# Attention with a relative bias and a squared-ReLU network on one core: v as fp32 by another queue, and one more batch turned by DMA

## The chip, the core and the metric

The kernel runs on one core of a Trainium2 chip. The metric is the device time of one execution, in microseconds (us); the time before is 378.62 us, the median of three runs (378.29 to 379.13). The profile is that of one execution, whose instructions span 376.3 us. The core's engines have these names in it: PE is TensorE (matrix multiplies; PEld is its loading of weights), ACT is ScalarE, DVE is VectorE, POOL is GpSimd and SP is SyncE, which here does nothing but issue transfers.

## The reference

Eight batches, eight heads, 576 positions, heads of 64. Attention with a bias that depends on the distance of two positions alone, then a layer 512 to 2048, a ReLU, a square, and a layer 2048 to 512, for all 4608 tokens:

```python
def _attn_ref(q, k, v, bias_table):          # (8, 8, 576, 64); table (32, 8); all fp32
    scores = scale * np.matmul(q, k.transpose(0, 1, 3, 2))
    bucket = ...                             # of |i - j|; one bucket from distance 128 on
    bias = bias_table[bucket]
    scores = scores + bias.transpose(2, 0, 1)[None, :, :, :]
    attn = np.exp(scores - max); attn = attn / (sum + 1e-09)      # cut: over the last axis
    return np.matmul(attn, v)

def _moe_ref(x, w_in, w_out):                # x (4608, 512), w_in (512, 2048), w_out (2048, 512)
    h = np.maximum(x @ w_in, 0.0)
    return h * h @ w_out
```

## The kernel before

The kernel works in fp16 with fp32 sums. Two heads make a *pair*: four pairs a batch, 32 in all. For each pair, q and k are laid with the head dimension on the partitions (they are *turned*), TensorE makes the scores (tile `st`), ScalarE takes exp (into `pt`, and `pm` for the last 64 keys), VectorE multiplies by the table of exp(bias) where it differs from a constant, TensorE multiplies by v (tile `pv`), and VectorE divides by the sums (tile `x`). x is turned again (into `xt`) for the network, which runs in nine *layers* of 512 tokens: f1 (L1044) with w_in, a ReLU into `rt`, a square into `g`, and f2 (L962) with w_out in seven products instead of eight, for which VectorE makes sums of quarters of the weights and of the activations.

All work is first entered in a plan, with estimated durations; a list scheduler puts it in order, and each engine's instructions are emitted in that order. So the order on every engine is fixed in the program, and constants that steer the plan (when a pair or a layer is due) change the order everywhere.

```python
DT_QK = 3                                    # q, k are turned by DMA from this batch on
PERIOD, LEAD, FAST, FASTN = 9600.0, 1600.0, 3000, 7      # when pair p is due, in planned ns
AHEAD, G0, GP = 20600.0, 54700.0, 35900.0    # layer g is due at G0 + GP * g
DT_X = 3                                     # x is turned by DMA from this batch on
RELU_DVE = 2                                 # in layers below this, VectorE may take a ReLU
SIX = 3                                      # batches below this: q, k loaded six rows to a partition
ORDER = "k0 i0 q0 q1 v i1 i2 o0 k1 o1 i3 o2 o3"   # q, k, v of batch 1 and the weights (i: w_in, o: w_out)
...
def nominal(p):
    return LEAD + FAST * min(p, FASTN) + PERIOD * max(p - FASTN, 0)
```

The loads are issued by GpSimd's queue, which casts fp32 to fp16 on the way. A pair of a batch below SIX is one transfer for q and one for k, with long rows; from SIX on it is three each, row by row, in the form that a DMA transpose takes. A batch of v is four transfers into `va` and two into `vm` (last 64 keys):

```python
def load_six(p, w):
    ... src.rearrange("h (p j) d -> p h (j d)", j=6) ...

def load_rows(p, w):
    ... [src[e, 0:512, :].rearrange("(t p) d -> p t d", p=128) for e in range(2)] ...
    ... [src[:, 512:S, :].rearrange("e p d -> p e d")] ...

def load_v(b):
    for tt in range(4):
        l = load("POOL", nc.gpsimd, lambda tt=tt: vas[b_v[b].slot][:, tt, :, 0:64],
                 const(v[b, :, ts(tt, 128), :].transpose([1, 0, 2])), ...)
    load_v_tail(b)                           # two transfers into vm
```

Turning q and k, and x:

```python
def pair(p):
    for w, dst in ((0, qts), (1, kts)):
        if b >= DT_QK:
            nc.sync.dma_start_transpose(out=dst[...], in_=stg[b_stg[p].slot][w][:, 0:640])   # by SyncE
            continue
        # else TensorE (L608), 12 transposes if b < SIX, into PSUM tile f
        nc.tensor.transpose(ps[ds(64 * e, 64), ts(j, 96)], six(t)[:, e, ts(j, D)], id_sb[0:96, 0:96])
        # and ScalarE or VectorE copies PSUM to qt / kt (L570, L572)
    # copies of the last 64 queries and keys into qz (L635): GpSimd, or for b < DT_QK VectorE or GpSimd
    ...
    if b >= DT_X:
        nc.sync.dma_start_transpose(out=xt_sb[...], in_=xs[...])        # 2 a pair, by SyncE

def x_turn(b, norms):                        # for b < DT_X, by TensorE (L848)
    for qt in range(5):
        for kk in range(4):
            nc.tensor.transpose(ps[:, ts(kk, 128)], xs[xb[kk].slot][:, qt, :], id_sb)
        # then a copy to xt by ScalarE or VectorE
```

Of the kernel before, what the change touches and what calls it, by code (L numbers as in the profile page):

```python
# [10 lines left out]
FP32 = mybir.dt.float32  # L11
# [6 lines left out]
B, H, S, D = 8, 8, 576, 64  # L18
# [8 lines left out]
NG = B * S // GT  # L27
XB = 3
XR = XB * S
DT_QK = 3  # L30
PERIOD, LEAD, FAST, FASTN = 9600.0, 1600.0, 3000, 7
AHEAD, G0, GP = 20600.0, 54700.0, 35900.0
DT_X = 3
RELU_DVE = 2
NSTG, NQK, NPT, NV, NX, NGB, NRT, NY = 5, 4, 3, 3, 6, 2, 4, 4
QUIET, LATER = 5200.0, 8500.0
TAB, EV = 6400.0, 1
P_ORDER = "1 6 2 5 7 3 4"
P_LAST = "1 6 2 5 7 3 4"
SIX = 3  # L40
ORDER = "k0 i0 q0 q1 v i1 i2 o0 k1 o1 i3 o2 o3"
HALF = GT // 2


# [133 lines left out]
def mm(n):  # L178
    return n / 2.4 + 2.5


def act(n):
    return 174.0 + n / 1.2


def dve(n, rate=1.0, fix=160.0):
    return fix + n / (0.96 * rate)
# [3 lines left out]
def kernel(  # L191
# [10 lines left out]
    nc = tc.nc  # L202
    assert (_bucket(np.arange(128, S)) == NBK - 1).all()

    def io(ins):
        tc.keep_in_program_order(ins)
        return ins
# [11 lines left out]
    def sb(name, shape, dtype=FP16):  # L219
        return single.tile(shape, dtype, name=name)  # L220
# [4 lines left out]
    w_out_sb = sb("w_out_sb", [128, 16, 512])  # L225
# [1 line left out]
    tm_sb = sb("tm_sb", [128, 4, 192])  # L227
    bt_sb = sb("bt_sb", [128, 8], FP32)
    far_sb = sb("far_sb", [1, 8], FP32)
    one_sb = sb("one_sb", [1, 128], FP32)  # L230
    ex_sb = sb("ex_sb", [128, 8])
    eb_sb = sb("eb_sb", [128, 4, 8])
    oh_sb = sb("oh_sb", [128, 512])
    stg = [[sb(f"{n}s{i}", [128, 12 * D]) for n in "qk"] for i in range(NSTG)]
    qts = [sb(f"qt{i}", [128, 640]) for i in range(NQK)]
    kts = [sb(f"kt{i}", [128, 640]) for i in range(NQK)]
# [6 lines left out]
    vas, v4s = ([t[:, i] for i in range(NV)] for t in (va_sb, vm_sb))  # L243
# [2 lines left out]
    wt_sb = sb("wt", [128, 3, 8, 256])  # L246
    ss = {i: sb(f"s{i}", [128, 8, 2, 128]) for i in (1, 2, 4)}
    gs = [sb(f"g{i}", [128, 16, GT]) for i in range(NGB)]
    rts = [sb(f"rt{i}", [128, GT]) for i in range(NRT)]
    ys = [sb(f"y{i}", [128, 512], FP32) for i in range(NY)]  # L250
    rs = [sb(f"r{i}", [128, 3, 2, 1], FP32) for i in range(2)]
# [5 lines left out]
    P = Plan()  # L257
# [5 lines left out]

    def loader(eng_name, eng, out_, in_, packets, deps=(), bufs=(), due=0.0):

        lane = [Buf(r_lane)] if eng_name == "POOL" else []
        issue = P.add(
            {eng_name: 720.0 if eng_name == "POOL" else 600.0},  # L270
            lambda: io(eng.dma_start(out=out_(), in_=in_())),  # L271
            deps,
            list(bufs) + lane,
            due,
        )
        return P.add({"DMA": packets / 16}, None, [issue], list(bufs) + lane, due if lane else -1e9), issue

    def one_of(engs, fn, deps, bufs, due):
        op = P.add(engs, None, deps, bufs, due)
# [3 lines left out]
    def const(f):  # L283
        return lambda: f

    def load(eng_name, eng, out_, in_, packets, deps=(), bufs=(), due=0.0):
        return loader(eng_name, eng, out_, in_, packets, deps, bufs, due)[0]


    first_f = gs[NGB - 1].bitcast(FP32).rearrange("p t c -> p (t c)")  # L290
# [6 lines left out]
        for w, (n, e, t) in enumerate((("SP", nc.sync, q), ("ACT", nc.scalar, k)))  # L297
# [22 lines left out]
        due=5,  # L320
# [20 lines left out]
                out=eb_sb, in0=sel_sb, in1=ex_sb.rearrange("p (a h) -> p a h", a=1).to_broadcast([128, 4, 8]), op=MULT  # L341
# [5 lines left out]
    for c in range(6):  # L347
# [11 lines left out]
        o = P.add({"PE": 16 * 55.0}, t_mm, [o_eb, l_oh], [t_b], LEAD + TAB, 0.0, "f")  # L359

        def t_ev(o, c=c, t_b=t_b):
# [4 lines left out]
            else:  # L366
# [8 lines left out]
                    out=tm_sb[ds(64 * e, 64), :, :], in_=tb_sb[ds(64 * e, 64), e::2, 64 * e : 64 * e + 192]  # L375
# [11 lines left out]
    def fill(ap, value, ns, due, after, deps=()):  # L387
        return P.add({"DVE": ns}, lambda: io(nc.vector.memset(ap, value)), deps, (), due, after)
# [7 lines left out]
    v_fix = [  # L396
        [
            o,
            fill(va_sb[:, a, :, :, 64:66], VSC, 150.0, 30, at),
            *(fill(vm_sb[ds(64 * e, 64), a, :, e, 64:66], VSC, 90.0, 30, at, [o]) for e in range(2)),  # L400
        ]
        for a, ns, at in ((slice(0, 1), 250.0, QUIET), (slice(1, NV), 500.0, LATER))
        for o in [fill(vm_sb[:, a].bitcast(FP32), 0.0, ns, 30, at)]
    ]
# [5 lines left out]

    b_v = [Buf(r_v) for _ in range(B)]
    l_qk = {}
    l_v = {}
    pool_due = [0.0]

    def pdue():
        pool_due[0] += 1.0
        return pool_due[0]  # L420
# [62 lines left out]
    def load_v_tail(b):  # L483
        for e in range(2):
            l = load(
                "POOL", nc.gpsimd,
                lambda e=e: v4s[b_v[b].slot][ds(64 * e, 64), :, e, 0:64],
                const(v[b, e::2, 512:576, :].transpose([1, 0, 2])),
                256 * 34.5, v_fix[min(b, 1)], [b_v[b]], pdue(),
            )  # L490
            for hp in range(4):
                l_v.setdefault((b, hp), []).append(l)

    def load_v(b):
        for tt in range(4):
            l = load(
                "POOL", nc.gpsimd,
                lambda tt=tt: vas[b_v[b].slot][:, tt, :, 0:64],
                const(v[b, :, ts(tt, 128), :].transpose([1, 0, 2])),
                1024 * 34.5, v_fix[min(b, 1)], [b_v[b]], pdue(),  # L500
            )
            for hp in range(4):
                l_v.setdefault((b, hp), []).append(l)
        load_v_tail(b)

    l_win, l_wout = [], []

    def load_w_in(u):
        l_win.append(
# [6 lines left out]
        )  # L516

    def load_w_out(u):
        l_wout.append(
            load(  # L520
                "POOL", nc.gpsimd,
                const(w_out_sb[:, 4 * u : 4 * u + 4, :]),
                const(moe_w_out[ds(512 * u, 512), :].rearrange("(a p) c -> p a c", p=128)),
                512 * 102, (), (), pdue(),
            )
        )

    for hp in range(4):
        for w in range(2):
# [9 lines left out]
    for h in range(6, 8):  # L539
        load_v_head(0, h)  # L540
    for step in ORDER.split():
        if step[0] == "i":
# [8 lines left out]
    for b in range(2, B):  # L551
        for p in range(4 * b, 4 * b + 4):
            for w in range(2):
                (load_six if b < SIX else load_rows)(p, w)
        load_v(b)

    def nominal(p):
        return LEAD + FAST * min(p, FASTN) + PERIOD * max(p - FASTN, 0)  # L560

    xt_ready, x_last = {}, {}
    x_bufs = {}
# [16 lines left out]
    def pair(p):  # L580
# [5 lines left out]
        for w, dst in ((0, qts), (1, kts)):  # L586
            if b >= DT_QK:
                o = P.add(
# [12 lines left out]
            def tr(w=w, bank=bank):  # L601
                ps = g_ps[bank.slot].bitcast(FP16)
                t = stg[b_stg[p].slot][w]
                if b < SIX:
                    for j in range(6):
# [10 lines left out]

            o = P.add({"PE": 12 * 36.0 if b < SIX else 5 * mm(128)}, tr, l_qk[p, w] + [l_id], [bank, b_stg[p]], T - 3000, after, "c" if b < SIX else "f")

            def turned(bank=bank):
                ps = g_ps[bank.slot].bitcast(FP16)[:, 0:S]  # L620
                return ps.rearrange("p (j t) -> p t j", j=6) if b < SIX else ps

            def straight(dst=dst):
                d = dst[qb.slot][:, 0:S]
                return d.rearrange("p (t j) -> p t j", j=6) if b < SIX else d

            evac.append(copy_to(S, straight, turned, [o], [bank, qb], T - 3000, b >= SIX, 0 < p < EV))
        spread = []
        for w, src, dst in ((0, qts, qzs), (1, kts, kzs)):
            for e in range(2):  # L630
# [5 lines left out]

                spread.append(one_of({"DVE": 200.0, "POOL": 320.0} if b < DT_QK else {"POOL": 320.0}, sp, [evac[w]] + z_fix[min(p, 1)], [qb], T - 1000))
        pb = Buf(r_pt)
# [132 lines left out]
        for part, qt0, nq in ((0, 0, 3), (1, 3, 2)):  # L771
# [48 lines left out]
            norms.append(o)  # L820
            if b >= DT_X:
                c = (b % XB) * S + 128 * qt0
# [61 lines left out]
    def sums_of_weights():  # L884

        done = []
        for c0 in (0, 4):
            cs = ds(c0, 4)
            l = [l_wout[c0 // 2], l_wout[c0 // 2 + 1]]
            t2, t3, t4 = (wt_sb[:, i, cs] for i in range(3))  # L890
            w11, w12, w21, w22 = (w4[:, cs, o, h] for o in range(2) for h in range(2))
            o = None
            for out_, a, b_, op in (
                (t3, w22, w12, mybir.AluOpType.add),
                (w12, w12, w11, mybir.AluOpType.subtract),
                (t2, w22, w12, mybir.AluOpType.add),
                (t4, w21, t2, mybir.AluOpType.subtract),
            ):
                o = P.add(
                    {"DVE": dve(1024, 2.0)},  # L900
                    lambda out_=out_, a=a, b_=b_, op=op: io(nc.vector.tensor_tensor(out=out_, in0=a, in1=b_, op=op)),
                    l + [o], (), 1e5,
                )
            done.append(o)
        return done
# [23 lines left out]
    def second(g):  # L929
# [22 lines left out]
        atoms = []  # L952
        for i in (int(x) for x in (P_LAST if g == NG - 1 else P_ORDER).split()):
            bk, left, right, ns = prod[i]
# [71 lines left out]
    def layers(g):  # L1026
# [27 lines left out]
        for i in range(16):  # L1054
            if i < len(atoms1):
# [12 lines left out]

                engs = {"ACT": act(512), "DVE": dve(512)} if g < RELU_DVE else {"ACT": act(512)}
                r = one_of(engs, relu, [o], [bank, rb], 0.0)  # L1070
# [26 lines left out]
    for b in range(B):  # L1097
        norms = [pair(4 * b + hp) for hp in range(4)]
        if b < DT_X:
            x_turn(b, norms)  # L1100
# [38 lines left out]
```

The softmax here doesn't subtract the row's maximum and nothing guards it: scores larger than these inputs give would overflow.

## Time and profile before

| what | value |
|---|---|
| time, median of 3 runs | 378.62 us |
| span of the profiled execution | 376.3 us |
| mean granted TensorE clock | 0.995 of full |
| transfers | 146163 packets, 38.74 MB |
| DMA issues by GpSimd for q and k | 142, some 0.72 us each |
| DMA issues by GpSimd for v | 36 of 0.86 us (va), 16 of 0.63 us (vm) |
| DMA transposes by SyncE | 40 for x, 20 each for q and k |

The page of a profile lists busy time by engine, then the span in 40 equal slices with a digit for tenths of busy time in each (9 is 90% or more). The view of waits lists who waited for whom: total, times, longest. The table of windows gives the busy time of each engine in stretches of the span. The timeline lists instructions in order of time: start, length, engine, line, what is written and read, count, and in brackets the idle time before and what ended it. A length there runs to the modelled end of the last matmul; matmuls overlap, so the time that a group occupies is better read from its start to the next start.

### The profile page before, as it was taken

What the parts mean: (1) busy time and instruction counts of PE and PEld (TensorE: products, weight loads), DVE (VectorE), ACT (ScalarE), POOL (GpSimd) and SP (SyncE); (2) the same over time, 40 slices, a digit from 0 to 9 for tenths busy, and PEclk for the clock granted to TensorE, in tenths of its full rate; (3) what the DMA queues carried; (4) which work ended last, traced back from release to release, by engine and by line L of the source; (5) the groups of instructions that cost most, each with busy time, mean ns of one, the idle gap of its engine ahead of it and who ended that gap; (6) DMA issues with size and microseconds to landing.
All of it is one profiled execution on the core that took longest, in us unless ns stands there. A gap on an engine that the chain in (4) does not pass through costs nothing.

```text
span 376.3 us, 10050 instructions
## 1 busy us (share of the span) xinstructions
PE 362.4 (96%) x4046; PEld 247.6 (66%) x4046; DVE 269.0 (71%) x612; ACT 255.5 (68%) x361; POOL 178.3 (47%) x318
## 2 busy tenths in 40 slices
PE   3988999999999999999999999999999999999996
PEld 2656555745778666687766765677577878556775
DVE  3987689998788677767685777757776683583653
ACT  4888979988557887866787778747885541564330
POOL 7876453889368583933758446583550000000000
PEclk9989999999999999999999999999999999999999
DMA  9999999699999999949999799999990222200103
GB/s 171 145 119 159 200 170 88 44 95 84 83 159 129 111 118 145 108 47 119 142 135 67 109 121 149 79 110 105 162 116 30 77 58 68 70 2 28 57 28 111
DMA packets 146163, 38.74 MB, mean 103 GB/s; under 512 B 128070, under 2 KB 146118, under 8 KB 146118
## 3 DMA queue, kind: packets, MB, share of 16 engines
q0 software_dynamic: 94496, 18.07, 60.9%
q1 hardware_dynamic: 51280, 19.75, 27.3%
q8 instruction: 31, 0.51, 0.6%
q10 hardware_dynamic: 342, 0.30, 0.3%
q14 instruction: 14, 0.11, 0.1%
HBM read 36.88 MB, written 9.44 MB: 123 GB/s over the span
## 4 chain that ended last, share of the span: by engine, by line
PE 90%; ACT 4%; DVE 3%; issue 1%; DMA 1%; ACTq 0%
PE f L1044 34%; PE f L962 29%; PE pv L788 10%; PE st L653 9%; PE pv L781 3%; PE st L702 2%; PE st L677 2%; ACT pt L664 1%; PE f L608 1%; DMA g<-in_k_dram 1%; ACT pt L687 1%; PE f L848 1%; DVE x L810 0%; ACT kt L570 0%; PE f L353 0%
## 5 line engine op out<-in xcount | busy, mean ns | idle before, releaser
L664 ACT ACTIVATE pt<-st 128x1024 f16<-128x1024 f32 x128 | 126.8, 1024 | 22.6 <-PE st L653 22.5
L1044 PE MATMUL f<-xt,w_in_sb 128*128 128x512 f16 (+4 forms) x704 | 142.1, 341 | 0.0
L1065 ACT ACTIVATE rt<-f 128x512 f16<-128x512 f32 x134 | 80.0, 598 | 62.0 <-PE f L1044 60.5
L1044 PEld LDWEIGHTS <-w_in_sb 128*128 128x128 f16 x704 | 62.6, 98 | 53.0 <-issue 10.8
L1075 DVE TENSOR_TENSOR g<-rt 128x512 f16<-128x512 f16 x144 | 60.7, 423 | 41.3 <-ACT rt L1065 40.2
L745 DVE TENSOR_TENSOR pt<-pt,tb_sb 128x1536 f16<-128x1536 f16 (+2 forms) x96 | 58.2, 621 | 10.6 <-ACT pt L664 10.2
L962 PEld LDWEIGHTS <-g 128*128 128x128 f16 x576 | 54.9, 98 | 15.4 <-issue 4.7
L788 PE MATMUL pv<-va,pt 128*128 128x65 f16 x1280 | 55.3, 194 | 0.0
L788 PEld LDWEIGHTS <-pt 128*128 128x128 f16 x1280 | 50.9, 98 | 2.9 <-issue 0.7
L271 POOL DMA_DIRECT2D qs<-in_q_dram x71 | 50.0, 725 | 2.4 <-DMA ks<-in_k_dram 1.1
L271 POOL DMA_DIRECT2D ks<-in_k_dram x71 | 50.0, 715 | 1.4 <-issue 1.4
L962 PEld LDWEIGHTS <-s 128*128 128x128 f16 x432 | 40.6, 98 | 10.6 <-issue 3.4
L635 POOL COPY qz<-qt 64x64 f16<-64x64 f16 x53 | 15.5, 293 | 64.2 <-DMA qt<-qs 35.5
L989 DVE SCALAR_TENSOR_TENSOR y<-f,y 128x512 f32<-128x512 f32 (+1 forms) x47 | 31.4, 667 | 16.1 <-PE f L962 15.1
L653 PE MATMUL st<-qt,kt 64*128 64x512 f16 x256 | 41.6, 396 | 1.1 <-ACT pt L664 0.5
L962 PE MATMUL f<-wt,g 128*128 128x256 f16 x288 | 36.6, 273 | 0.0
L962 PE MATMUL f<-w_out_sb,s 128*128 128x256 f16 x288 | 36.6, 273 | 0.0
L962 PE MATMUL f<-w_out_sb,g 128*128 128x256 f16 x288 | 36.2, 273 | 0.1
L781 PE MATMUL pv<-vm,pm 128*128 128x130 f16 x160 | 35.5, 222 | 0.5 <-DVE x L810 0.4
L635 POOL COPY qz<-kt 64x64 f16<-64x64 f16 x59 | 20.2, 342 | 33.3 <-DMA kt<-ks 17.4
L810 DVE TENSOR_TENSOR x<-pv,r 128x384 f16<-128x384 f32 x64 | 31.4, 490 | 1.9
L271 POOL DMA_DIRECT2D va<-in_v_dram x36 | 30.8, 860 | 1.5 <-DMA qs<-in_q_dram 0.8
(62 smaller groups left out, 308.0 us busy)
## 6 DMA issues: line engine op xcount, KB each, us to landing
out_dram<-y SPq DMA_DIRECT2D x34, 256.0 KB, 2.4
va<-in_v_dram POOLq DMA_DIRECT2D x28, 128.0 KB, 4.7
qs<-in_q_dram POOLq DMA_DIRECT2D x40, 64.0 KB, 3.2
ks<-in_k_dram POOLq DMA_DIRECT2D x40, 64.0 KB, 3.0
w_in_sb<-in_moe_w_in_dram POOLq DMA_DIRECT2D x4, 512.0 KB, 7.6
w_out_sb<-in_moe_w_out_dram POOLq DMA_DIRECT2D x4, 512.0 KB, 9.9
qs<-in_q_dram POOLq DMA_DIRECT2D x11, 144.0 KB, 5.0
ks<-in_k_dram POOLq DMA_DIRECT2D x11, 144.0 KB, 6.2
```

What stands on the lines that cost most here:

```text
L271: lambda: io(eng.dma_start(out=out_(), in_=in_())),
L635: io(eng.tensor_copy(out=dst[qb.slot][rw, rw], in_=src[qb.slot][rw, 512:576]))
L653: nc.tensor.matmul(sets_ps[st.slot][:, e, :], kt[rw, ts(jt, 128)], qt[rw, 0:512], start=True, stop=True,)
L664: nc.scalar.activation(out=p5(pts[pb.slot])[:, jt, :, 0:512], in_=sets_ps[st.slot], func=EXPF, scale=SCALE)
L745: io(nc.vector.tensor_tensor(out=a, in0=a, in1=t, op=MULT))
L781: nc.tensor.matmul(ps[:, i, :, :], pm[:, c : c + 128], vm[:, hp, :, 0:65], start=True, stop=False)
L788: nc.tensor.matmul(ps[:, i, e, :], pt[:, (2 * jt + e) * S + c : (2 * jt + e) * S + c + 128], va[:, jt, 2 * hp + e, 0:65], start=False, sto ...
L810: nc.vector.tensor_tensor(out=xs[xb.slot][:, qt0 : qt0 + nq, :].rearrange("p t (e d) -> p t e d", e=2), in0=ps[:, :, :, 0:64], in1=rs[rb.s ...
L962: nc.tensor.matmul(g_ps[bf.slot][:, ts(s_, HALF)], left(c, s_), right(c), start=(c == 0 and (s_ == 0 or apart) and i not in before), stop= ...
L1044: nc.tensor.matmul(g_ps[bank.slot][:, a:z], w_in_sb[:, kk, ts(nt, 128)], xt_sb[:, kk, c : c + z - a], start=(kk == 0), stop=(kk == 3),)
L1065: io(nc.scalar.activation(out=rts[rb.slot], in_=g_ps[bank.slot], func=RELUF))
L1075: nc.vector.tensor_tensor(out=gs[gb1.slot][:, nt, :], in0=rts[rb.slot], in1=rts[rb.slot], op=MULT)
```

## The change

From batch 2 on, v no longer goes through GpSimd's queue. SyncE's queue fetches it as fp32 into two new buffers of 128x512, and GpSimd copies it from there into `va` and `vm` as fp16. The first of these loads is held until the last weights' load has been issued: GpSimd writes a column of each buffer behind that issue, and the load waits for it. What this relieves is spent on one more batch turned by DMA: q, k (DT_QK) and x (DT_X) of batch 2, whose q and k are then loaded row by row (SIX). The ReLUs of the first two layers go to ScalarE alone (RELU_DVE). Two small tiles used at the start move into the room of `g0`, the sums of weights are made in quarters instead of halves, and the constants of the plan and the order of the loads are set anew.

```diff
-DT_QK = 3
-PERIOD, LEAD, FAST, FASTN = 9600.0, 1600.0, 3000, 7
-AHEAD, G0, GP = 20600.0, 54700.0, 35900.0
-DT_X = 3
-RELU_DVE = 2
-NSTG, NQK, NPT, NV, NX, NGB, NRT, NY = 5, 4, 3, 3, 6, 2, 4, 4
-QUIET, LATER = 5200.0, 8500.0
-TAB, EV = 6400.0, 1
-P_ORDER = "1 6 2 5 7 3 4"
+DT_QK = 2
+PERIOD, LEAD, FAST, FASTN = 8500, 2000.0, 3300.0, 6
+AHEAD, G0, GP = 24600.0, 60000, 39000.0
+DT_X = 2
+RELU_DVE = 0
+NSTG, NQK, NPT, NV, NX, NGB, NRT, NY, NF = 5, 4, 3, 3, 6, 2, 4, 4, 2
+QUIET, LATER = 5000.0, 9000
+TAB, EV = 2700.0, 1
+P_ORDER = "1 2 6 5 7 3 4"
 P_LAST = "1 6 2 5 7 3 4"
-SIX = 3
-ORDER = "k0 i0 q0 q1 v i1 i2 o0 k1 o1 i3 o2 o3"
+SIX = 2
+V_EARLY, V_HW = 18900.0, 2
+T_POOL, T_DUE = 0, 0
+ORDER = "k0 i0 q1 q0 v i1 o0 k1 i2 o1 o2 i3 o3"
...
-    one_sb = sb("one_sb", [1, 128], FP32)
-    oh_sb = sb("oh_sb", [128, 512])
+    oh_sb = gs[0][:, 0, :]
+    one_sb = gs[0].bitcast(FP32)[0:1, 2, 0:128]
+    fs = [sb(f"f32{i}", [128, 512], FP32) for i in range(NF)]
...
+    r_f = Ring(NF, True)
+
+    def load_v_fp32(b):
+
+        due, at = pdue(), max(0.0, nominal(4 * b) - V_EARLY)
+        held = []
+        if b == V_HW:
+
+            held = [
+                P.add({"POOL": 60.0}, lambda t=t: io(nc.gpsimd.memset(t[:, 0:1], 0.0)), [i_wout[-1]], (), due)
+                for t in fs
+            ]
+        for tt in range(5):
+            fb = Buf(r_f)
...          # tt < 4: one part, fs[...] <- v[b, :, ts(tt, 128), :], then va; tt == 4: two halves, then vm
+            for room, src, dst, packets, ns in parts:
+                l = load("SP", nc.sync, room, const(src), packets, held, [fb], due, after=at, turn=due)
+                o = P.add(
+                    {"POOL": ns},
+                    lambda room=room, dst=dst: io(nc.gpsimd.tensor_copy(out=dst(), in_=room())),
+                    [l] + v_fix[1], [fb, b_v[b]], due,
+                )
...
-        load_v(b)
+        (load_v_fp32 if b >= V_HW else load_v)(b)
...
-        for c0 in (0, 4):
-            cs = ds(c0, 4)
-            l = [l_wout[c0 // 2], l_wout[c0 // 2 + 1]]
+        for c0 in range(0, 8, 2):
+            cs = ds(c0, 2)
+            l = [l_wout[c0 // 2]]
```

More of the change, by code (lines that the diff above doesn't have):

```diff
@@ L262, with loader @@
     r_s = {i: Ring(1) for i in (1, 2, 4)}
-    def loader(eng_name, eng, out_, in_, packets, deps=(), bufs=(), due=0.0):
+    def loader(eng_name, eng, out_, in_, packets, deps=(), bufs=(), due=0.0, after=0.0, turn=-1e9):
         lane = [Buf(r_lane)] if eng_name == "POOL" else []
@@ L274, in loader @@
             due,
+            after,
         )
-        return P.add({"DMA": packets / 16}, None, [issue], list(bufs) + lane, due if lane else -1e9), issue
+        return P.add({"DMA": packets / 16}, None, [issue], list(bufs) + lane, due if lane else turn), issue
     def one_of(engs, fn, deps, bufs, due):
@@ L284, in const, with load @@
         return lambda: f
-    def load(eng_name, eng, out_, in_, packets, deps=(), bufs=(), due=0.0):
-        return loader(eng_name, eng, out_, in_, packets, deps, bufs, due)[0]
+    def load(*args, **kw):
+        return loader(*args, **kw)[0]
     first_f = gs[NGB - 1].bitcast(FP32).rearrange("p t c -> p (t c)")
@@ L409, with nominal @@
     ]
+    def nominal(p):
+        return LEAD + FAST * min(p, FASTN) + PERIOD * max(p - FASTN, 0)
     b_v = [Buf(r_v) for _ in range(B)]
@@ L504, in load_v @@
         load_v_tail(b)
-    l_win, l_wout = [], []
+    r_f = Ring(NF, True)
[9 more added lines that the diff above has]
+            fb = Buf(r_f)
+            if tt < 4:
+                parts = [
+                    (
+                        lambda fb=fb: fs[fb.slot].rearrange("p (h d) -> p h d", h=H),
+                        v[b, :, ts(tt, 128), :].transpose([1, 0, 2]),
+                        lambda tt=tt: vas[b_v[b].slot][:, tt, :, 0:64],
+                        1024 * 19, 760.0,
+                    )
+                ]
+            else:
+                parts = [
+                    (
+                        lambda e=e, fb=fb: fs[fb.slot][ds(64 * e, 64), 0:256].rearrange("p (h d) -> p h d", h=4),
+                        v[b, e::2, 512:576, :].transpose([1, 0, 2]),
+                        lambda e=e: v4s[b_v[b].slot][ds(64 * e, 64), :, e, 0:64],
+                        256 * 19, 420.0,
+                    )
+                    for e in range(2)
+                ]
+            for room, src, dst, packets, ns in parts:
[4 more added lines that the diff above has]
+                    [l] + v_fix[1], [fb, b_v[b]], due,
+                )
+                for hp in range(4):
+                    l_v.setdefault((b, hp), []).append(o)
+    l_win, l_wout, i_wout = [], [], []
     def load_w_in(u):
@@ L518, in load_w_out @@
     def load_w_out(u):
[L519 to L525, printed above, removed]
-        )
+        l, issue = loader(
+            "POOL", nc.gpsimd,
+            const(w_out_sb[:, 4 * u : 4 * u + 4, :]),
+            const(moe_w_out[ds(512 * u, 512), :].rearrange("(a p) c -> p a c", p=128)),
+            512 * 102, (), (), pdue(),
+        )
+        l_wout.append(l)
+        i_wout.append(issue)
     for hp in range(4):
@@ L554 @@
                 (load_six if b < SIX else load_rows)(p, w)
-        load_v(b)
-    def nominal(p):
-        return LEAD + FAST * min(p, FASTN) + PERIOD * max(p - FASTN, 0)
+        (load_v_fp32 if b >= V_HW else load_v)(b)
     xt_ready, x_last = {}, {}
@@ L899, in sums_of_weights @@
                 o = P.add(
-                    {"DVE": dve(1024, 2.0)},
-                    lambda out_=out_, a=a, b_=b_, op=op: io(nc.vector.tensor_tensor(out=out_, in0=a, in1=b_, op=op)),
-                    l + [o], (), 1e5,
+                    {"POOL": 1150.0} if T_POOL else {"DVE": dve(512, 2.0)},
+                    lambda out_=out_, a=a, b_=b_, op=op: io(
+                        (nc.gpsimd if T_POOL else nc.vector).tensor_tensor(out=out_, in0=a, in1=b_, op=op)
+                    ),
+                    l + [o], (), T_DUE if T_POOL else 1e5,
                 )
```

## The prediction

> **What bounds the kernel now.** I began with the page's first two parts, busy time and the span in 40 slices of 9.4 us.
>
> ```profile
> PE 362.4 (96%) x4046; PEld 247.6 (66%) x4046; DVE 269.0 (71%) x612; ACT 255.5 (68%) x361; POOL 178.3 (47%) x318
> PE   3988999999999999999999999999999999999996
> DMA  9999999699999999949999799999990222200103
> ```
>
> TensorE is busy 96% of the span, and its digit is 9 from the fifth slice to the last but one. DMA is at 9 for most of the first 280 us, so two resources look full. Which one ends waits? The view of waits, TensorE alone:
>
> ```profile
> PE f L608 <- DVE ks L470: 5.9, 1, 5.9
> PE st L702 <- ACT pt L664: 0.8, 1, 0.8
> PE f L848 <- DVE x L810: 0.6, 1, 0.6
> ```
>
> The 5.9 us are the start, before the first keys are there; nothing else exceeds 0.8 us, and no DMA is among the releasers. The DMA engines are busy but not waited for by TensorE (one weight load apart, below). The table of windows says where the idle time lies (columns: start:end, length, then busy time and count of PE, PEld, DVE, ACT and POOL, then clock, DMA share, GB/s):
>
> ```profile
> 0.00:10.00 10.00, 4.11 (x66) 3.01 (x66) 3.94 (x17) 4.74 (x7) 8.08 (x18) 1.00 0.95 173
> 10.00:20.00 10.00, 9.27 (x164) 5.90 (x160) 9.12 (x24) 8.71 (x12) 8.63 (x17) 1.00 1.52 147
> 20.00:30.00 10.00, 9.15 (x172) 6.50 (x169) 8.39 (x29) 9.00 (x13) 7.48 (x15) 0.83 1.30 109
> 30.00:40.00 10.00, 8.04 (x149) 5.83 (x143) 7.42 (x21) 8.52 (x13) 7.33 (x14) 1.00 1.11 179
> 60.00:80.00 20.00, 19.74 (x290) 12.64 (x288) 18.93 (x47) 19.10 (x31) 12.92 (x26) 1.00 0.77 51
> 360.00:377.00 17.00, 12.57 (x113) 10.77 (x111) 7.28 (x13) 1.79 (x3) 0.00 (x0) 0.96 0.19 64
> ```
>
> Idle TensorE time is 376.3 - 362.4 = 13.9 us: 9.4 in the first 40 us (40 - 4.11 - 9.27 - 9.15 - 8.04), 3.7 at the end (16.3 - 12.57), under 1 between. A busy TensorE needn't be at its peak, so I checked starts in its timeline: from 41.24 us, where the first layer's matmuls begin, twelve f1 matmuls of 512 columns start 2.70 us before what follows them, and eight f2 matmuls of 256 columns occupy 0.87 us wherever they follow one another. That is near what the columns cost, next paragraph. So there are two stages. Up to 41 us the four head pairs of batch 0 run and ScalarE sets the pace (8.5 to 9.0 of 10 us); from 41 to 373 us TensorE works through a fixed list with no slack, and only what leaves that list shortens it.
>
> **What the Trainium skill says.** "TensorE: Matmul & The Clock Gate", section "Wait — 56ns, not 53.3ns?", gives N/2.4 GHz plus about 2.5 ns between warm matmuls: 8 x (256/2.4 + 2.5) = 873 ns. The trace has 0.87 us, so it agrees. "DMA: Bandwidth & Descriptors", section "SWDGE vs HWDGE vs iDMA", says a casting DMA must come from GpSimd and a transposing one from SP or ACT; the before has exactly this split (v, fp32 to fp16, by GpSimd; DMA_TRANSPOSE by SP). That is why fp32 v on SyncE's queue needs a cast elsewhere. "GPSIMD Engine Reference", section 3.1 (Elementwise), has 512 elements in 769 ns for a tight one-input loop, and section 1 says GpSimd shares its SBUF interfaces with VectorE. This trace has GpSimd copies only of 64x64, 293 to 342 ns, so neither the long cast nor the contention is shown here.
>
> **The change, part by part.** *Turns of q and k, batch 2.* The 24 groups of twelve transposes (144 transposes each for q and k) go by pair, two groups each; counting them off, the first 16 are over by 51 us and the last eight, batch 2's, stand at 63.9 to 72.1 us, inside the full stage. Timeline, TensorE lines:
>
> ```profile
> 63.94 0.45 PE L608 MATMUL f<-id_sb,qs 96*64 96x96 f16 x12
> 64.22 0.42 PE L608 MATMUL f<-id_sb,ks 96*64 96x96 f16 x12
> 64.58 0.80 PE L653 MATMUL st<-qt,kt 64*128 64x512 f16 x4
> ...
> 69.83 0.45 PE L608 MATMUL f<-id_sb,ks 96*64 96x96 f16 x12
> 70.21 0.23 PE L781 MATMUL pv<-vm,pm 128*128 128x130 f16 x1
> ```
>
> Two groups occupy 63.94 to 64.58 = 0.64 us; the matmul before should have let go at about 63.85 (these pv groups of nine repeat every 0.30, of which the last eight take 0.24), so a switch of 0.09 goes with them: 0.73. The next two, 65.31 to 66.08 and the wait before them: 0.96. A single one at 68.92 ends at 69.30, with its lead 0.48; at 69.83, 0.38; the last two, 71.45 to 72.09 and lead, 0.74. Sum 0.73 + 0.96 + 0.48 + 0.38 + 0.74 = 3.3 us. (Just before 69.83 a weight load waits 0.42 us, put down to a vm load. I don't count it.)
>
> *Turns of x, batch 2.* 20 transposes, at 117.55, 119.47 and 120.32:
>
> ```profile
> 117.55 0.61 PE L848 MATMUL f<-id_sb,x 128*128 128x128 f16 x8
> 118.00 0.22 PE L781 MATMUL pv<-vm,pm 128*128 128x130 f16 x1
> ```
>
> From start to next start 0.45, then 0.32 and 0.46: 1.2 us. So the list loses 4.5 us on the path.
>
> *Beside the path.* Eight evacuations qt/kt (0.67 ScalarE, 0.75 VectorE) and five xt ones (0.60 and 0.42 at full size) go: near 8 us of ScalarE and VectorE, most of it around 64 to 73 us, where both are over 90% busy. The ten ReLUs on VectorE (0.69 each) go to ScalarE (0.60 each, 6 us). No weight here after 80 us.
>
> *GpSimd.* Batches 2 to 7 leave its queue: 24 va issues of 0.88 and 12 vm of 0.63 = 28.7 us. Casts come instead, estimated from the page above: 24 x 0.77 + 12 x 0.39 = 23 us. Batch 2's q and k by rows need 24 issues for 8, 16 x 0.65 = +10 us. So it goes from 178 to about 183 us: no bound.
>
> *SyncE.* 36 loads and 16 more transposes (1.2 us of issue each): 19 us plus the loads at the 0.4 of an out issue or more, some 15 to 20. From about 60 to 300 us that queue has room, but it is in order: a load waiting for a free fp32 buffer holds the transposes behind it.
>
> *DMA.* The software queue's 94496 packets are 60.9% of 16 engines' span, 0.609 x 376.3 x 16 / 94496 = 38.8 ns each; the hardware queue's 51280 at 27.3% are 32.1 ns. Batch 2 by rows has 8 x 1152 packets for 8 x 192, +7680 x 38.8 / 16 = +19 us; v's 27648 packets at the hardware price, -27648 x 6.7 / 16 = -12 us; and 16 transposes are new. The total stays about where it was, but more of it falls between 40 and 75 us.
>
> *The opening.* Tables come sooner (TAB 6400 to 2700), the order of the weights' loads and all pace constants change. Nothing removes a whole stage before 41 us; filling half of ScalarE's holes there (about 1.3 of each 10 us) would bring 1 to 2 us. I allow 1.5 gained there, and 0.6 lost to new waits of a static order whose transfers come at other times. Sum: 378.6 - 3.3 - 1.2 - 1.5 + 0.6 = 373.2 us.
>
> **The rivals.** (1) *Batch 2 comes late.* Its rows, v and transposes crowd into 40 to 75 us with the weights; each engine's order is fixed, so TensorE stops at its scores or its pv. For it: DMA is at 9 in those slices, and a transpose takes some 4 us to land where the PSUM copy took 0.7. Against it: the seventh and eighth slices and GpSimd's 8.2 and 6.6 us of idleness before 51.4 and 65.5 us are room, and layers 0 and 1 are work that needs no batch 2. With it: 3 to 7 us lost, 376 to 381. (2) *SyncE or GpSimd becomes a chain*: load, cast, buffer free, next load, with only two buffers; transposes stuck behind. For it: 6 loads of v and 16 transposes a batch on one ordered queue, and casts slowed by VectorE. Against it: 34 us a batch (the plan's 8.5 us a pair) for about 16 x 1.2 + 6 x 0.6 + 4 = 27 us of issue. With it: a loss in every batch, 382 or more. (3) *Only the opening counts*: the transposes hide in time TensorE would lose anyway. For it: the waits of 0.2 beside them. Against it: the neighbours are back to back. With it: 376 to 378. (4) *The opening gains more*, the first layer starts at 37 instead of 41 us: 370 to 371.
>
> **Range and chances.** The 4.5 us are the firm part; the opening may give -1 to 4, waits may take 0 to 5. That makes 369.5 to 378.5 for 8 in 10. Over 2% means below 371.05: the removed work alone misses it by 3 us, so it needs the fourth rival, 0.24. Over 2% slower is above 386.2 and needs the second rival in full strength: 0.05. The constants look chosen together with the parts, which keeps that low. Within 2%: 0.71.
>
> **What would show it.** Right: transposes L608 192 for 288 and L848 40 for 60, TensorE's busy sum near 358, its digits still 9 from the fifth slice on, casts of 0.8 us or so, first f1 matmul at 38 to 41 us. Wrong: TensorE waits of over 1 us on kt, qt or va between 50 and 90 us (first rival); SyncE's own queue waiting on casts, with transposes later from batch to batch (second); a first f1 beyond 43 us or before 37 (my opening). The prediction fails most easily in the opening, since its order comes out of constants and I have no durations for the new one.

## The result, and the profile after

The changed kernel takes 374.0 us (median of 4 runs, 373.57 to 374.7), before in the same runs 378.46 us: a ratio of 0.9885, 95% interval 0.986 to 0.991, so 4.4 us or 1.15% less. 373.2 us was predicted. The profiled execution spans 371.8 us against 376.3.

The page of the changed kernel, busy time and slices:

```profile
PE 355.6 (96%) x3930; PEld 242.2 (65%) x3930; DVE 264.4 (71%) x593; ACT 258.1 (69%) x368; POOL 184.1 (50%) x343
PE   3978999899999999999999999999999999999996
DMA  9999999797999999998999999999975122100103
```

TensorE has 116 matmuls less (96 turns of q and k, 20 of x) and its busy sum is 6.8 us lower; it is still at 9 from the fifth slice on, but for one dip to 8 in the eighth. GpSimd went from 178.3 to 184.1 us. The transfers' time went from 88.2% of 376.3 us (60.9 and 27.3) to 92.1% of 371.8 us (50.4 by GpSimd's queue, 41.7 by SyncE's). The signs named in advance: 192 transposes of q and k, 40 of x, a first f1 at 38 to 41 us, all as forecast; TensorE's busy sum was to be near 358 us and is 355.6, and the large casts take 0.68 us for 0.8.

TensorE's waits in the changed kernel:

```profile
PE f L656 <- ACT qs L476: 6.0, 1, 6.0
PE f L896 <- DVE x L858: 1.3, 3, 0.6
PE st L750 <- ACT pt L712: 1.3, 2, 0.8
PE pv L829 <- DVE x L858: 1.0, 3, 0.4
PE f L1012 <- ACT y L1045: 0.7, 1, 0.7
```

Again none on DMA. The waits on x grew from 1.0 to 2.3 us, the one on y is new, and the timeline shows where most of them lie:

```profile
38.98 2.76 PE L1094 MATMUL f<-xt,w_in_sb 128*128 128x512 f16 x12
...
65.72 1.91 PE L1012 MATMUL f<-w_out_sb,g 128*128 128x256 f16 x16 [0.68 <-ACT y L1045]
...
69.77 0.68 PE L896 MATMUL f<-id_sb,x 128*128 128x128 f16 x9 [0.44 <-DVE x L858]
...
71.78 0.45 PE L896 MATMUL f<-id_sb,x 128*128 128x128 f16 x5 [0.32 <-DVE x L858]
...
72.69 1.02 PE L1094 MATMUL f<-xt,w_in_sb 128*128 128x512 f16 x4 [0.24 <-ACT xt L618]
```

The first layer starts at 38.98 us, 2.26 us sooner than before; between 65 and 73 us TensorE loses some 1.7 us, where VectorE is busy 9.5 of 10 us (60 to 70 us).

The same 542 matmuls stand ahead of the first f1 in both kernels, so the span can be divided there. The table of windows for the two parts, before and then the changed kernel (start:end, length, busy time and count of PE first, TensorE's granted clock third from the end):

```profile
0.00:41.24 41.24, 31.48 (x542) 21.64 (x543) 29.44 (x89) 32.15 (x44) 32.34 (x61) 0.96 1.22 153
41.24:376.30 335.06, 330.89 (x3506) 225.91 (x3504) 239.59 (x523) 223.32 (x318) 145.92 (x257) 1.00 0.85 97
```

```profile
0.00:38.97 38.97, 28.39 (x542) 20.04 (x542) 28.91 (x87) 31.67 (x44) 32.82 (x65) 1.00 1.29 158
38.97:371.80 332.83, 327.16 (x3390) 222.19 (x3388) 235.45 (x506) 226.45 (x325) 151.24 (x279) 1.00 0.89 114
```

From the first layer on TensorE is busy 3.7 us less and idle 1.5 us more (5.7 for 4.2).

The casts that GpSimd took over, from the groups of instructions (count, busy sum and mean in ns, idle time before):

```profile
L551 POOL CAST va<-f 128x512 f16<-128x512 f32 x24 | 16.2, 676 | 8.1 <-DMA f<-in_v_dram 7.3
L551 POOL CAST vm<-f 64x256 f16<-64x256 f32 x12 | 6.5, 542 | 10.4 <-DMA f<-in_v_dram 10.2
```

### The profile page after: what moved, and what is told of

It is laid out like the page before. It is cut to its first block, busy times and chain, and to the rows that moved or that the text cites. A ratio compares the mean times of both kernels' runs of the same rounds, so it can differ in the third digit from the quotient of the medians.

```text
span 371.8 us, 9912 instructions
## 1 busy us (share of the span) xinstructions
PE 355.6 (96%) x3930; PEld 242.2 (65%) x3930; DVE 264.4 (71%) x593; ACT 258.1 (69%) x368; POOL 184.1 (50%) x343
## 3 DMA queue, kind: packets, MB, share of 16 engines
q0 software_dynamic: 74208, 14.53, 50.4%
q1 hardware_dynamic: 87696, 28.80, 41.7%
## 4 chain that ended last, share of the span: by engine, by line
PE 85%; DVE 8%; DMA 3%; ACT 2%; issue 1%; SPq 0%; POOL 0%; ACTq 0%; DVEq 0%
PE f L1094 33%; PE f L1012 28%; PE pv L836 8%; PE st L701 8%; PE pv L829 2%; DMA kt<-ks 2%; PE st L750 2%; DVE pt L793 2%; PE st L725 1%; DMA g<-in_q_dram 1%; DVE x L858 1%; DVE s L971 1%; PE f L656 1%; ACT pm L760 1%; DVE kt L620 1%
## 5 line engine op out<-in xcount | busy, mean ns | idle before, releaser
L1094 PE MATMUL f<-xt,w_in_sb 128*128 128x512 f16 (+4 forms) x704 | 138.6, 341 | 0.2 <-ACT xt L618 0.2
L1115 ACT ACTIVATE rt<-f 128x512 f16<-128x512 f32 x144 | 85.2, 602 | 49.3 <-PE f L1094 45.3
L1125 DVE TENSOR_TENSOR g<-rt 128x512 f16<-128x512 f16 x144 | 63.3, 444 | 37.0 <-ACT rt L1115 36.1
L793 DVE TENSOR_TENSOR pt<-pt,tb_sb 128x1536 f16<-128x1536 f16 (+2 forms) x96 | 61.2, 646 | 14.9 <-ACT pt L712 14.3
L275 POOL DMA_DIRECT2D qs<-in_q_dram x79 | 55.4, 715 | 5.3 <-DMA w_out_sb<-in_moe_w_out_dram 2.6
L275 POOL DMA_DIRECT2D ks<-in_k_dram x79 | 55.2, 702 | 1.3 <-issue 1.1
L1012 PEld LDWEIGHTS <-s 128*128 128x128 f16 x432 | 41.1, 98 | 10.6 <-issue 2.8
L701 PE MATMUL st<-qt,kt 64*128 64x512 f16 x256 | 40.3, 385 | 0.8 <-ACT pt L735 0.4
L683 POOL COPY qz<-qt 64x64 f16<-64x64 f16 x61 | 17.4, 285 | 42.0 <-DMA qt<-qs 35.7
L683 POOL COPY qz<-kt 64x64 f16<-64x64 f16 x58 | 19.2, 331 | 37.0 <-DMA kt<-ks 28.3
L971 DVE TENSOR_TENSOR s<-g,s 128x1024 f16<-128x1024 f16 x36 | 25.0, 693 | 0.4
```

The lines of the kernel that those rows point to most:

```text
L683: io(eng.tensor_copy(out=dst[qb.slot][rw, rw], in_=src[qb.slot][rw, 512:576]))
L701: nc.tensor.matmul(sets_ps[st.slot][:, e, :], kt[rw, ts(jt, 128)], qt[rw, 0:512], start=True, stop=True,)
L793: io(nc.vector.tensor_tensor(out=a, in0=a, in1=t, op=MULT))
L1012: nc.tensor.matmul(g_ps[bf.slot][:, ts(s_, HALF)], left(c, s_), right(c), start=(c == 0 and (s_ == 0 or apart) and i not in before), stop= ...
L1094: nc.tensor.matmul(g_ps[bank.slot][:, a:z], w_in_sb[:, kk, ts(nt, 128)], xt_sb[:, kk, c : c + z - a], start=(kk == 0), stop=(kk == 3),)
L1115: io(nc.scalar.activation(out=rts[rb.slot], in_=g_ps[bank.slot], func=RELUF))
```

## The experiments

In step with the prediction I call it the *list theory* that TensorE's list is the bound from 41 us on, so that only what leaves it counts. Its rival at first was that relief of DMA pays: v on the other queue. Every kernel ran beside the kernel before on its chip, and I compare ratios; 1% is 3.8 us. Ratios leave out executions that the chip ran in a slower state, so where a kernel's ratio and its median disagree (v back, v as fp32 by GpSimd), the ratio is the better figure. A caution holds for all: an edit of a constant lets the plan order everything anew, so a difference of a few tenths of a percent can come from the order.

### The two halves of the change, each alone and each undone

*Turns back.* The changed kernel, batch 2 turned by TensorE again:

```diff
-DT_QK = 2
-DT_X = 2
-SIX = 2
+DT_QK = 3
+DT_X = 3
+SIX = 3
```

> The kernel after, with batch 2's q, k and x turned by TensorE again (DT_QK, DT_X, SIX = 3); v stays on SyncE's queue and the new constants stay. List theory (TensorE's list is the bound from 41 us on; what left it is the gain): the 4.5 us come back, 377 to 379 us, the first layer still starts at 39 us. Rival, relief of DMA (v on the other queue is what pays): 374 to 375 us, as after.

Measured 380.36 us, ratio 1.0063 (1.0039 to 1.0088). Against 0.9885 that is 1.8% or 6.7 us dearer, so the 4.5 us come back and 2 more. The first layer starts at 39.50 us, and from 60 to 90 us TensorE idles 2.9 us (after: 1.7) at a mean granted clock of 0.89, so part of the 2 us is the clock in this execution. The direction is the list theory's.

*Turns alone.* The kernel before, with DT_QK, DT_X and SIX set to 2 and nothing else.

> The kernel before, with only the turns of batch 2 given to DMA (DT_QK, DT_X, SIX = 2); v by GpSimd, old constants. List theory: 4.5 us off TensorE's list, 1 to 3 us of new waits where rows and transposes come late: 375 to 377 us, first layer at 41 us. Rival, relief of DMA: rows add about 19 us of DMA work between 40 and 75 us with nothing to make room, TensorE waits there for more than it saves, 379 us or more.

Measured 394.63 us, ratio 1.0448 (1.0418 to 1.0477). The list theory fails by 18 us.

*v back.* The changed kernel, with v as before:

```diff
-V_EARLY, V_HW = 18900.0, 2
+V_EARLY, V_HW = 18900.0, 8
```

> The kernel after, with v of all batches cast by GpSimd's DMA again (V_HW = 8), all else as after. List theory: the same TensorE list, so 374 to 376 us, with waits of at most 2 us more. Rival, relief of DMA: v, 12 us of DMA work more in all and 52 issues back in GpSimd's queue, makes batch 2 and later ones late: 378 us or more, waits of TensorE on pt or kt beyond 60 us.

Median 389.58 us, ratio 1.0259 (1.0211 to 1.0307), which is about 387 us. TensorE has the same list as in the changed kernel, and the time is 3.8% longer.

*v alone.* The changed kernel, with turns, constants and load order of before (and the sums of weights in quarters, which stay).

> The kernel after with the turns, the constants and the load order of before: only v's way by SyncE and GpSimd's cast stays new (and sums of weights in quarters). List theory: nothing leaves TensorE's list, 378 to 379.5 us as before. Rival, relief of DMA: 374 to 376 us.

Measured 379.49 us, ratio 1.0045 (1.0028 to 1.0061): v's move alone brings nothing, rather a loss of 0.45%. From 60 to 90 us TensorE idles 2.6 us.

Taken together: the turns alone cost 4.5%, v alone 0.45%, v and the new constants without the turns 0.6%, the turns and the new constants without v's move 2.6%; all of it saves 1.15%. So neither theory holds alone. What TensorE gains comes from its list; what v's move brings is that this gain can be had. Two combinations were not run: the new constants alone, and both halves with the old constants. Nor were the constants set anew for turns without v's move, so that a better order could make up for v's way there is neither shown nor excluded.

The table of windows from 140 to 320 us shows what happens without v's move (PE is the first sum, DMA share the last number but one). The changed kernel, turns alone, v back (its execution of 388.12 us, below), and v back with an edit described below:

```profile
140.00:320.00 180.00, 179.57 (x2064) 128.72 (x2061) 128.80 (x277) 128.30 (x181) 90.06 (x169) 1.00 0.94 123
```

```profile
140.00:320.00 180.00, 169.47 (x1844) 117.09 (x1843) 116.97 (x255) 123.49 (x175) 101.84 (x179) 0.97 1.06 107
```

```profile
140.00:320.00 180.00, 170.02 (x1938) 120.32 (x1937) 119.47 (x262) 123.28 (x174) 96.59 (x172) 0.99 0.99 107
```

```profile
140.00:320.00 180.00, 172.02 (x1989) 122.22 (x1988) 130.16 (x332) 127.20 (x179) 60.83 (x84) 1.00 0.84 99
```

TensorE idles 0.4, 10.5, 10.0 and 8.0 us of 180. In the last its granted clock is 1.00 and DMA is at 0.84, below the changed kernel's 0.94, so the loss needs neither a lower clock nor busier DMA engines. The chain of waits of the same stretch, changed kernel, then v back (the view ends there):

```profile
by line: PE f L1094 34.1%; PE f L1012 33.7%; PE pv L836 12.1%; PE st L701 9.9%; DMA kt<-ks 4.5%; PE pv L829 3.2%; PE st L750 2.3%; PE st L725 2.0%; POOL qz L683 0.5%; issue 0.1%
```

```profile
by line: PE f L1094 27.3%; PE f L1012 23.1%; PE pv L836 10.6%; PE st L701 6.6%; ACT pt L712 4.0%; DMA kt<-ks 3.1%; ACT rt L1115 3.1%; PE pv L829 3.1%; DVE s L971 3.0%; DVE pt L793 2.3%; DMA xt<-x 2.3%; PE st L750 2.2%; issue 2.0%; PE st L72
```

TensorE's lines make up 97% of the chain in the changed kernel (its 4.5% of turning k are one piece that begins at 136.09 us, ahead of the stretch) and some 73% in v back, as far as its line goes. What fills the rest there is every step of a pair and a layer in turn, turning k and x, exp, the tables, ReLU, sums; no single link stands out. In another execution of v back, of 393.62 us, turning k had 13.3%. The pairs come too slowly: the scores of the last 64 keys (L750) of the 16th, 20th, 24th and 28th pair start at 148.10, 189.88, 233.73 and 276.69 us, some 43 us a batch; in the changed kernel at 140.05, 182.48, 221.52 and 260.56, some 40.

### What of v's move it is: DMA time or GpSimd's queue

*v twice.* The changed kernel, with every large v transfer issued by SyncE a second time into memory that nothing reads. The order on TensorE, ScalarE, VectorE and GpSimd is the same as in the changed kernel.

```diff
+idle_d = nc.dram_tensor("idle_d", [B, 4, 128, H, D], FP32, kind="Internal").ap()
 ...
+# right behind each load of 128 rows of v, by the same queue
+nc.sync.dma_start(out=idle_d[b, tt], in_=src)
```

> The kernel after, with each of the 24 large v transfers from batch 2 on issued a second time by SyncE, into a spare place in memory that nothing reads: only the load on SyncE's queue and the DMA engines is doubled, the order on all other engines is the same. DMA theory (in turns_only and v_back the DMA engines' time was what ran out): 24 x 1024 packets at 32 ns over 16 engines are 49 us of DMA work more in some 230 us that are 90% busy; TensorE falls short of work between 140 and 320 us, 385 us or more. Queue theory (it was GpSimd's ordered queue, with v's issues between those of q and k): 374 to 377 us, since GpSimd's queue is untouched.

Measured 378.01 us, ratio 1.0019 (1.0 to 1.0039): 1.3% or 5 us over the changed kernel. From 140 to 320 us:

```profile
140.00:320.00 180.00, 178.48 (x2062) 127.48 (x2062) 129.71 (x279) 128.65 (x180) 90.53 (x171) 1.00 1.05 146
```

The DMA engines moved 146 GB/s instead of 123, and TensorE lost 1.5 us instead of 0.4. The 49 us were too high an estimate: by the pages the transfers of SyncE's queue take 48.2% of 376.2 us for 41.7% of 371.8, some 26 us more. They cost 5 us, between the two expectations; of the 4.4 us between the two profiles 1.3 are there before the first doubled load, with a dip of TensorE's clock (last section). That is far from the 14 us of v back, whose DMA share of 0.99 is lower. DMA time is not free, but it isn't what made v back slow.

*v as fp32 by GpSimd.* The changed kernel, with the issuing queue of the fp32 loads exchanged. The plan's time for these transfers is doubled and their turn in it dropped, and they now count among the eight loads that the plan lets GpSimd have under way:

```diff
-l = load("SP", nc.sync, room, const(src), packets, held, [fb], due, after=at, turn=due)
+l = load("POOL", nc.gpsimd, room, const(src), 2 * packets, held, [fb], due, after=at)
```

> The kernel after, with the fp32 loads of v issued by GpSimd's queue instead of SyncE's; no cast on the way, GpSimd casts as in after. DMA theory: the packets cost about what they do in after, 374 to 378 us. Queue theory: GpSimd's queue has the issues and the casts, 28 and 23 us, in one order, 385 us or more.

Measured 405.33 us, ratio 1.0657 (1.0593 to 1.0721), which is about 402 us. The same bytes, no cast by DMA, a DMA share of 0.89 from 140 to 320 us in the profiled execution, and 7.8% over the changed kernel: what decides is the queue that issues v, or the order that the plan makes of it, not the packets' form.

*v back again, and with the qz copies on VectorE.* The obvious wait in GpSimd's queue is that of the copies into qz, which wait for DMA turns, between load issues. In v back, GpSimd's waits:

```profile
POOL qz L683 <- DMA kt<-ks: 44.5, 13, 8.6
POOL qz L683 <- DMA qt<-qs: 44.1, 12, 10.3
```

First v back once more, on the chip of the next run:

> The kernel of v_back once more (v of all batches cast by GpSimd's DMA), one look, as the neighbour of the next run: 385 to 392 us, GpSimd waiting some 60 us on qt and kt between its load issues.

A single execution took 388.12 us, GpSimd waiting 44.9 + 43.4 us for kt and qt. Then with that wait taken out of GpSimd's queue:

```diff
-{"DVE": 200.0, "POOL": 320.0} if b < DT_QK else {"POOL": 320.0}
+{"DVE": 200.0, "POOL": 320.0} if b < DT_QK else {"DVE": 200.0}
```

> The kernel of v_back, with the copies into qz made by VectorE instead of GpSimd from batch 2 on, so that nothing in GpSimd's queue waits for a DMA transpose any more. Queue theory (the waits for qt and kt stand in one order with the issues of loads and hold them up): the loads come sooner and most of the 15 us over after is won back, 376 to 381 us. DMA theory (the packets of casting loads are the limit): 386 us or more.

Measured 386.62 us, ratio 1.0261 (1.022 to 1.0302): on balance nothing is won, and the 376 to 381 us of my queue theory in its narrow form are missed. The edit doesn't only free GpSimd's queue, it also loads VectorE: in the changed kernel, below, the same edit costs 1.6%, so some 6 us may have been won here and spent again. GpSimd's waits show what else stands in the way:

```profile
POOL qs L275 <- DMA qt<-qs: 62.9, 11, 9.8
POOL ks L275 <- DMA kt<-ks: 18.4, 7, 6.7
```

The copies gone, the load issues themselves wait for the same turns: a load needs a staging buffer, and the turn of an earlier pair frees it. And SyncE, which issues the turns in order, waits elsewhere. SyncE's own waits from 140 to 320 us in v back with qz on VectorE:

```profile
SPq L874 <- DVE r L853: 71.3, 9, 17.8
```

and in the changed kernel:

```profile
SPq L874 <- DVE x L858: 13.1, 7, 5.8
...
SPq L874 <- DVE r L853: 9.0, 5, 2.7
```

L874 turns x. It waits for VectorE's normalization, which waits for pv, which waits for this pair's q, k and v; and behind it in the queue stand the next turns of q and k, which free the buffers for the next loads. As I read these waits it is a ring: load, turn, scores, pv, turn of x, next turn, next load. Where it is held differs: in v as fp32 by GpSimd SyncE waits longest, 74.3 us from 140 to 320 us, for y (L1065), since the stores of the results stand in the same queue. Moving v off GpSimd's queue shortens one link of the ring. Whether the link is the issue time (28.7 us over the kernel) or the order that the plan gives when it must fit v's issues in between, these runs don't tell apart, since each of the three slow kernels also has a new order; I leave that open.

*The changed kernel with qz on VectorE*, the same edit:

> The kernel after, with the copies into qz made by VectorE from batch 2 on. Queue theory: GpSimd no longer waits for transposes, but with v off its queue the pairs already come in time; TensorE's list is the same, 373 to 375 us; VectorE has 48 pairs of copies of 0.2 us more, some 20 us. If GpSimd's queue still costs something in after: 371 to 372.5 us.

Measured 378.72 us, ratio 1.0039 (1.0026 to 1.0053), 1.6% over the changed kernel. GpSimd's busy sum falls from 184 to 157 us and VectorE's rises from 264 to 281; TensorE idles 3.1 us from 60 to 100 us (1.7 in the changed kernel). What the edit takes from GpSimd doesn't make up for what it asks of VectorE; what a freer queue of GpSimd would be worth by itself it doesn't show.

### The opening, the hold, and the stretch at 65 us

*Tables' date.* The changed kernel with `TAB` 6400 for 2700.

> The kernel after, with the tables' due time as before (TAB 6400 instead of 2700). If the earlier tables are what brings the first layer forward from 41.2 to 39.0 us: it starts at 41 us and the time is 376 us. Rival (pace constants and load order do it): 39 us, 374 us.

Measured 375.29 us, ratio 0.9954 (0.9926 to 0.9983), first layer at 39.74 us. That is 0.7% over the changed kernel, and the first layer starts 0.8 us later, between the two expectations. Since some 1.3 of the 2.26 us go with TensorE's clock (last section), little of them is left for pace constants and load order; but the edit changes the order too.

*No hold.* The changed kernel without GpSimd's two writes behind the last weights' issue; the order is the same on every engine.

```diff
-if b == V_HW:
+if False:
     held = [ ... nc.gpsimd.memset(t[:, 0:1], 0.0) ... ]
```

> The kernel after without the hold: GpSimd's two writes behind the last weights' issue are gone, so SyncE issues the first two v loads as soon as its queue comes to them; the order on all engines is otherwise the same. If the hold guards the opening: two loads of 1024 packets, 4 us of DMA work, fall among the loads of batches 0 and 1 and the weights, first layer 1 us later, 375 to 376 us. Rival (only two transfers can slip forward with two buffers): 374 us, no difference that can be told.

Measured 376.57 us, ratio 0.9984 (0.9967 to 1.0001), 1.0% over the changed kernel. SyncE now issues the two loads at 2.15 us, and TensorE's timeline shows who pays:

```profile
16.52 0.41 PE L750 MATMUL st<-qt,qz 128*128 128x288 f16 x2 [0.47 <-ACT pt L712]
18.20 0.23 PE L829 MATMUL pv<-vm,pm 128*128 128x130 f16 x1 [1.28 <-DMA vm<-in_v_dram]
```

The first pv waits 1.28 us for batch 0's own v, and the first layer starts at 40.25 us. The hold earns its place.

*Sums of weights later.* In the changed kernel VectorE makes them from 44 to 74 us, ten of the sixteen from 62 us on, in the very stretch where TensorE waits on x. The plan may place them from 74 planned us on only:

```diff
-    l + [o], (), T_DUE if T_POOL else 1e5,
+    l + [o], (), T_DUE if T_POOL else 1e5, 74000.0,
```

> The kernel after, with the sums of weights on VectorE planned for no earlier than 74 us instead of 62 to 73 us. If VectorE's full stretch from 61 to 73 us is what makes TensorE idle 1.7 us there: 372.3 to 373.2 us, and no waits of TensorE on x or xt there. Rival (those waits come from the pairs' own chain): 374 us.

Measured 374.76 us, ratio 0.9935 (0.9911 to 0.9959): no gain, rather 0.5% lost. They are made from 68 to 83 us. VectorE's busy time from 60 to 70 us falls from 9.5 to 8.3 us, but TensorE's idle time from 60 to 90 us only from 1.7 to 1.4: the waits on x fall from 0.8 to 0.3 us, the longest, 0.7 us on ScalarE's y, stays. (The first layer starts at 40.06 us, with the dip of the clock described in the last section.) So VectorE's full stretch explains a part of the waits at most; that the rest is the pairs' own chain is not shown.

No run beats the changed kernel.

## Why the prediction was right, and where it wasn't

**Bound.** Held: TensorE's list from the first layer on, no wait on DMA, the busy digits as before.

**Turns.** 3.3 + 1.2 = 4.5 us were to leave the list. From the first layer on TensorE's busy time fell by 3.7 us. Undoing the turns costs 6.7 us, of which some 1.2 are more idle time at 60 to 90 us and a part is the clock; the term is of the right size, though not measured finer than a microsecond or two, since the order changes with it.

**Opening.** 1.5 us were allowed, 2.26 shown by the profile. But the kernel of v twice, in the same order, starts its first layer at 40.25 us, so about 1.3 us of this varies from execution to execution (below), and 1 us is left. The reason given, filling ScalarE's holes, fits in kind: in the first 40 us ScalarE is busy 32.7 us for 31.0. TensorE's idle time ahead of the first layer did not shrink (10.6 us for 9.8); the same 542 matmuls took 3.1 us less, 1.5 of them by the clock (29.89 us in v twice).

**New waits.** 0.6 us were allowed. The idle time after the first layer's start grew from 0.4 to 2.5 us (1.7 at 60 to 90, 0.4 each in 140 to 320 and 340 to 360 us), so 2.1. I mis-sized this term: they are the waits on x and y at 65 to 73 us, where the prediction itself had noted ScalarE and VectorE over 90% busy, and I had counted only what leaves that stretch. The tail is 0.6 us shorter (3.1 for 3.7). Sum of the spans: -2.3 - 3.7 + 2.1 - 0.6 = -4.5, as measured. Against the prediction's terms the opening gave 0.8 us more and the list 0.8 less, waits took 1.5 more and the tail 0.6 less: that the total came within 0.8 us is in part luck.

**GpSimd and DMA.** "From 178 to about 183 us: no bound" was right in its number (184.1) and poor as a reason. In the number two errors cancel: the casts were estimated at 0.77 and 0.39 us and took 0.68 and 0.54, 22.7 us in all for 23. In v back GpSimd is busy 191 of 386 us, and in turns alone 193 of 393: no more than half, and yet the supply of pairs fails. What failed is the step from a busy sum to "no bound": the queue is in order and part of a ring. I had priced v's move at nothing on the path, and it is worth 14 us once batch 2 is turned by DMA. The total came out since the changed kernel has both.

**Rivals.** (1) batch 2 late by DMA: no such wait in the changed kernel. (Of the two slices of room named against it only the eighth was one; in the seventh DMA stood at 9.) (2) SyncE or GpSimd as a chain, 382 us or more: absent in the changed kernel; turns alone, v back and v as fp32 by GpSimd (387 to 402 us) show a loss of this size. (3) only the opening counts: turns back speaks against it, its first layer starts at 39.5 us and it is slower than before. (4) a first layer at 37 us: it came at 39.

## What to carry to other kernels

A transfer moved to another queue may be worth nothing by itself and be the condition for another change: price such pairs together, and test each half alone. Where ordered queues feed each other's buffers, a busy share of 50% doesn't clear an engine; ask what stands behind what, and expect that a wait taken away in one place may come back at the next link. An edit that moves work to free one engine also loads another: measure what it costs where the wait is absent. Then compare where the work that the bound engine needs arrives, batch by batch.

## What the runs showed of the hardware that I had not expected

TensorE's granted clock differs between executions of one order of instructions. In the table of windows from 20 to 32 us (the last three columns are clock, DMA share, GB/s), the changed kernel, then v twice, whose order on TensorE is identical and whose first doubled load comes later, at 38.98 us:

```profile
20.00:32.00 12.00, 9.74 (x192) 6.82 (x191) 11.34 (x37) 10.96 (x15) 10.00 (x21) 1.00 1.41 135
```

```profile
20.00:32.00 12.00, 10.47 (x189) 7.32 (x186) 10.23 (x34) 9.79 (x14) 9.08 (x18) 0.86 1.37 132
```

At 0.86 TensorE is busier with three matmuls less, and the first layer starts 1.27 us later (40.25 for 38.98). The kernel before had such a dip as well (0.83 from 20 to 30 us), so part of the 2.26 us of its opening is this and not the change.

GpSimd's casts lengthen a few of VectorE's two-input operations. The squares before and in the changed kernel (shortest, median and longest in ns):

```profile
L1075 DVE TENSOR_TENSOR g<-rt x144: 394/424/458, 43.1 to 360.8; 128x512 f16<-128x512 f16 x144
```

```profile
L1125 DVE TENSOR_TENSOR g<-rt x144: 377/424/829, 41.3 to 356.5; 128x512 f16<-128x512 f16 x144
```

The median stays; thirteen squares take 513 to 829 ns, and each of them overlaps a cast. The mean is 423 to 426 ns in the kernels without casts (before, turns alone, the three runs with v back) and 427 to 454 with them (444 in the changed kernel, some 3 us in all). The Trainium skill's page "GPSIMD Engine Reference", section 1, names this shared interface; these runs show its size here.
